# Splitting and reordering the opening of a fused attention and expert kernel: loads, beta, weight scaling, the layout of k and the eps step

## The chip, the cores and the metric

The kernel runs on one core of one Trainium2 chip. A core has a matrix engine (TensorE, "PE" in the profile, with its weight loads as "PEld"), a vector engine (VectorE, "DVE"), an activation engine (ScalarE, "ACT"), a general engine (GpSimd, "POOL") and a queue engine (SyncE, "SP"), which here issues nearly all DMA transfers. Each engine works through its own instructions in order and waits on semaphores of the others. The metric is the device time of one execution in microseconds, median over several runs. Before the change it is 108.06 us (7 runs, 107.44 to 110.72).

## The reference

Two things are computed in a row. First a linear attention with a sketched feature map, for 4 batches of 4 heads with 1088 tokens of 32 values: phi(x) is the outer product of S1 x and S2 x (8 values each, so 64 features).

```python
q_p, k_p = (phi(q), phi(k))
kv = np.einsum('bhsf,bhsd->bhfd', k_p, v)
z = np.sum(k_p, axis=2)
num = np.einsum('bhsf,bhfd->bhsd', q_p, kv)
den = np.einsum('bhsf,bhf->bhs', q_p, z)[..., None] + 1e-06
return (num / den).astype(np.float32)
```

Then the 4352 tokens of 128 values (4 heads side by side) go through one expert of width 2048 with a swish that has a beta for each hidden unit.

```python
h = x @ w_in
g = h * (1.0 / (1.0 + np.exp(-beta * h)))
return (g @ w_out).astype(np.float32)
```

The kernel uses that h · sigmoid(beta h) = silu(beta h) / beta: it multiplies w_in by beta (winp) and w_out by 1/beta (woutp), once, and needs only a plain silu on ACT.

## The kernel before, in words

Tokens lie on partitions in 34 groups t of 32 tokens for each head (32 partitions a head). For k the 34 groups are padded to 36 = 4 x 9, and one DVE or POOL instruction forms the outer products of some of the 9 "outers" j for all heads at once.

**Expert.** `w1` (from L332) makes a wave: four matmuls of 256 tokens, or two of 512, into a PSUM buffer of two banks (pool `psm`, two buffers that take turns), then one ACT silu to g. `w2` (from L308) multiplies g by woutp and sums 16 units of 128 into moeout. The 2048 hidden values are these 16 units. The first 512 tokens go in two chunks of 256, the rest in chunks of 512. A wave of 256 tokens takes four units, so units 8 to 15 are first needed by the third wave.

**Batch 0** is handled by its own path, since nothing can overlap before it. Its q tokens come in two chunks, A (16 groups, the first 512 tokens) and B (18 groups). The steps: `turn_k`, `turn_q` transpose k and q on DVE; `kps` projects k with S1 and S2 on PE; `kab` transposes that back; `outer` forms phi(k) as kp; `gram`, `gram_terms`, `gram_z` build z (in zb0); `kv` sums k_p times v over the 9 outers in KVZ; `spread` on PE makes the repeated a and b factors of q (aps, bps), `asb` copies aps to SBUF on ACT, and `mult` multiplies them to qp on DVE; `den0` makes the denominators dps; `invert` transposes them (dT), adds 1e-6 and takes the reciprocal (rc); `spread_rc` spreads it by a transpose (rb); `num0` makes the numerators nps; `divide0` writes xT, the expert's input. Chunk B repeats spread, mult, den0, invert, num0 and divide0 as the steps aB, bB, mB, dB, iB, nB, xB.

**Weights.** beta is broadcast over the partitions by four PE matmuls with a matrix of ones (L247), copied to beta_bc by ACT (L251), and POOL multiplies w_in by it in eight steps of 256 columns (L258). rbeta = 1/beta comes from a PE transpose and a DVE reciprocal; ACT multiplies w_out by it, unit by unit (L273).

**What sets the order.** Every engine's order is written out by hand: first the straight-line code from L675 to L736, then the string SEQ (L828), whose tokens call small steps: W is a wave, V its second half, tk1, kp1, ka1 and so on are the steps of batch 1. `rest` runs the waves that are left. SP's queue is also in the order of the code: k in two parts, the early q part (chunk A), four loads of v, the first half of w_out and of w_in, the late q part (chunk B), k of batch 1, and the second halves. A DMA issue waits for the one that used the same of eight completion semaphores before it. `gate` is a tiny POOL copy that makes POOL wait for a DVE result before it starts a long multiply. `keep_warm` issues matmuls without use.

Of the kernel before, what the change touches and what calls it, by code (L numbers as in the profile page):

```python
# [9 lines left out]
F32 = mybir.dt.float32  # L10
# [4 lines left out]
P = 128  # L15
# [3 lines left out]
def kernel(  # L19
# [25 lines left out]
    TH = T // 2  # L45
    TPAD = 4 * NJK
    TCH = 512
# [8 lines left out]
    JR = [(0, 2), (2, 4), (4, 6), (6, 9)]  # L56
    WARM0 = 9

# [93 lines left out]

    def load_win(c0, c1):
        nc.sync.dma_start(out=w_in_sb[:, c0:c1], in_=moe_w_in[:, c0:c1])

    def load_wout(j0, j1):
        nc.sync.dma_start(
            out=w_out_sb[:, j0:j1, :],
            in_=moe_w_out[j0 * P : j1 * P, :].rearrange("(j p) m -> p j m", p=P),
        )  # L160
# [5 lines left out]
    load_v(0)  # L166
    load_wout(0, NJ // 2)
    load_win(0, DFF // 2)
    load_rows(q, q_t, 0, "q", ((QA0, T),))
    load_rows(k, k_t, 1, "k")  # L170
    load_win(DFF // 2, DFF)
    load_wout(NJ // 2, NJ)
    load_rows(q, q_t, 1, "q")
# [36 lines left out]
    for n in range(2):  # L210
        qT2.append(sb([P, T, 32], F32, f"qT{n}"))
        kT2.append(sb([P, TPAD, 32], F32, f"kT{n}"))
        nc.gpsimd.memset(kT2[n][:, T:, :], 0.0)
    zb0 = sb([P, H, 32], F32, "zb0")
# [12 lines left out]
    def prep_s(n):  # L227
        st_ = sb([P, 4, R], F32, f"st{n}")
        nc.vector.transpose(out=st_.rearrange("p u r -> p (u r)"), in_=sr[n])
        nc.gpsimd.tensor_tensor(out=sk[:, n], in0=st_[:, :2, :], in1=hm, op=MUL)  # L230
        t = sb([P, R, R], F32, f"s{n}")
        nc.scalar.copy(out=t, in_=cut(st_, ([[1, R], [0, R]], [[0, R], [1, R]])[n]))
        sab.append(t.rearrange("p i j -> p (i j)"))
        if n == 1:
            nc.gpsimd.tensor_tensor(
                out=s2h, in0=cut(sr[1], [[0, H], [1, D]]), in1=cut(mh, [[1, H], [0, D]]), op=MUL
            )


    beta_bc = sb([P, DFF], F32, "beta_bc")  # L240

    bq = [psm.tile([P, 2, 512], F32, tag="wave", name="betaps")]
    bq.append(ps1.tile([P, 512], F32, tag="one", name="betaps"))
    bq.append(pso.tile([P, 512], F32, tag="moeout", name="betaps"))
    for n, t in enumerate((bq[0][:, 0], bq[0][:, 1], bq[1], bq[2])):
# [3 lines left out]
    def beta_out(n):  # L249
        dst = beta_bc[:, (0, 1024, 1536)[n] : (1024, 1536, 2048)[n]]  # L250
        nc.scalar.copy(out=dst, in_=bq[n] if n else bq[0].rearrange("p a b -> p (a b)"))  # L251

# [3 lines left out]

    def prep_win(c0, c1, eng=None):
        (eng or nc.gpsimd).tensor_tensor(  # L258
            out=winp[:, c0:c1], in0=w_in_sb[:, c0:c1], in1=beta_bc[:, c0:c1], op=MUL
        )  # L260

    def prep_rbeta():
        bt = ps1.tile([P, 512], F32, tag="one", name="bt")
# [112 lines left out]


    def turn_k(b, t0=0, t1=T):
        nc.vector.transpose(  # L379
            out=kT2[b % 2][:, t0:t1].rearrange("p t s -> p (t s)"),  # L380
            in_=k_t[b][:, t0:t1].rearrange("p t d -> p (t d)"),
        )

# [8 lines left out]
    def wave2(name):  # L392
        return psm.tile([P, 2, 512], F32, tag="wave", name=name)
# [4 lines left out]
    def one(name):  # L398
        return ps1.tile([P, 512], F32, tag="one", name=name)
# [14 lines left out]
    def kps(b):  # L414
        t = PS["kps"] = two("kps")
        kT = kT2[b % 2]

        project(t, lambda rows, n: kT[rows, :, 8 * n : 8 * n + 8])

# [14 lines left out]
    def kab(b):  # L434
        KAB[b] = turn_ab(PS["kps"], "kab", [[8, NJK], [1, 8], [8 * NJK, 4]])

# [24 lines left out]

    def spread(which, n, dsts):
        t0, tn = q_chk[n]
        for c in range(2):
            for m in range(2):
                for pr, dst in enumerate(dsts):
                    h = 2 * pr + m
                    rows = slice(32 * h, 32 * h + 32)
                    nc.tensor.matmul(  # L469
                        out=dst[64 * c : 64 * c + 64, m, : 32 * tn],  # L470
                        lhsT=(sa if which == "a" else sb_)[rows, :],
                        rhs=qT2[0][rows, t0 + c * tn : t0 + c * tn + tn, :],
                        start=True,
                        stop=True,
                    )

# [58 lines left out]

    def kv(b, j_list):
        for j in j_list:
            for h in range(H):
                nc.tensor.matmul(  # L539
                    out=KVZ[b][32 * h : 32 * h + 32, :F],  # L540
                    lhsT=v_t[b][:, h, j, :],
                    rhs=KP[b][:, j, h, :],
                    start=(j == 0),
                    stop=(j == NJK - 1),
                    skip_group_check=True,
                )


    def gram(b):
        PS["gram"] = t = one("gram")  # L550
# [50 lines left out]

    def invert(dps, nn, tn):
        dT = sbA.tile([P, NJK, 32], F32, tag="dT", name="dT")
        nc.vector.transpose(out=dT[:, :tn].rearrange("p t c -> p (t c)"), in_=dps[:, : 32 * tn])
# [124 lines left out]
    num0(0, nps)  # L729
    keep_warm(2)  # L730
    for c in range(256, DFF, 256):
        prep_win(c, c + 256)
    for j in range(NJ // 2):
        prep_wout_act(j)
    for c in range(2):
        divide0(0, nps, spread_rc(rc, c, 8, 1), c, c + 1)  # L736


    def a_B():
        PS["a"] = [wave2("aps"), two("aps")]  # L740
        keep_warm(2, PS["a"][1][:, 0])
        spread("a", 1, PS["a"])
# [39 lines left out]

    DO = {"W": first, "V": second}
    for i in range(NJ // 4, NJ // 2):
# [9 lines left out]
    for b in range(1, B):  # L794
# [74 lines left out]
```

## Time and profile before

| | |
|---|---|
| median of 7 runs | 108.06 us |
| profiled execution | 108.21 us, span 106.0 us |
| PE busy | 96.4 us (91%) |
| ACT busy | 78.2 us (74%) |
| DVE busy | 66.3 us (63%) |
| POOL busy | 26.3 us (25%) |
| granted PE clock, mean | 0.992 |
| first expert wave starts | 16.91 us |
| first wave of batch 1's tokens starts | 30.88 us |

The page gives one profiled execution; times in the views count from the start of its span. A line of a timeline has the start, the duration, the engine, the source line, the operation, what it writes and reads, and in brackets how long the engine was idle before it and what ended that. A line of the chain of waits has the start, the length and the work that the end depended on at that time; "issue" is time in which nothing visible was waited for. In the rows by shape the columns are: line, engine, operation, output and input with their shapes, count; then busy time and mean nanoseconds of one; then the idle time before them with its releasers. A row of a DMA issue ends in the size of one and the time from issue to landing. PE's matmuls are pipelined, so their durations overlap and a busy PE is not a PE at its peak.

### The profile page before, as it was taken

The numbers are of one execution on the slowest core, as the hardware profiler recorded it, in microseconds if no ns is written. First come the engines' busy times: TensorE is split into PE (matmuls) and PEld (weight loads), VectorE is DVE, ScalarE is ACT, GpSimd is POOL, SyncE is SP. The second block draws the span as 40 slices with busy tenths as digits, with TensorE's granted clock in tenths as the row PEclk, the third lists the DMA queues.
The fourth block names the chain that finished last, engine by engine and source line by source line (L and its number), as shares of the span: only waits on it lengthen the run. The fifth ranks groups of instructions, "written<-read, shape, count | busy, mean of one in ns | idle before, by whom it ended". The sixth has DMA issues, their size and how long they took to land.

```text
span 106.0 us, 2880 instructions
## 1 busy us (share of the span) xinstructions
PE 96.4 (91%) x1175; PEld 46.2 (44%) x1175; DVE 66.3 (63%) x131; ACT 78.2 (74%) x102; POOL 26.3 (25%) x37
## 2 busy tenths in 40 slices
PE   6998966898979999999999999999899999999940
PEld 2335523355546643443454344337344444445720
DVE  5668759499899953997999654879945100200210
ACT  0755185839897985679987199799892999999920
POOL 5410029821059500400670044007400000000000
PEclk9999999999999999999999999999999999999996
DMA  3989999972002300028900463410014041023053
GB/s 79 320 249 301 371 353 386 384 242 69 6 0 50 53 6 0 0 42 117 343 23 12 74 147 89 74 25 6 0 22 77 0 74 31 0 40 62 11 88 50
DMA packets 24580, 11.33 MB, mean 107 GB/s; under 512 B 18900, under 2 KB 23028, under 8 KB 24568
## 3 DMA queue, kind: packets, MB, share of 16 engines
q1 hardware_dynamic: 23808, 11.05, 38.1%
q8 instruction: 9, 0.15, 0.6%
q10 hardware_dynamic: 696, 0.09, 0.5%
q0 software_dynamic: 64, 0.02, 0.1%
q14 instruction: 3, 0.02, 0.1%
HBM read 8.93 MB, written 2.23 MB: 105 GB/s over the span
## 4 chain that ended last, share of the span: by engine, by line
PE 54%; ACT 16%; DVE 11%; DMA 8%; SPq 5%; issue 2%; DVEq 0%; ACTq 0%
PE wave L341 19%; PE moeout L316 19%; ACT g L350 16%; DMA q<-in_q_dram 8%; PE nps L655 4%; PE kvz L539 3%; SPq L134 2%; PE kps L406 2%; PE yps L510 2%; DVE qT L385 2%; PE qps L406 1%; SPq L120 1%; DVE rb L614 1%; DVE xT L634 1%; PE bps L469 1%
## 5 line engine op out<-in xcount | busy, mean ns | idle before, releaser
L350 ACT ACTIVATE g<-wave 128x1024 f16<-128x1024 f32 x68 | 65.1, 1036 | 13.3 <-PE wave L341 13.0
L341 PE MATMUL wave<-xT,winp 128*128 128x512 f16 (+1 forms) x160 | 39.7, 347 | 2.8 <-DVE xT L634 2.2
L316 PE MATMUL moeout<-g,woutp 128*128 128x512 f16 (+1 forms) x160 | 38.6, 347 | 0.3 <-ACT g L350 0.3
L341 PEld LDWEIGHTS <-winp 128*128 128x128 f16 x160 | 14.5, 98 | 19.1 <-issue 9.2
L316 PEld LDWEIGHTS <-woutp 128*128 128x128 f16 x160 | 15.0, 97 | 16.1 <-issue 3.5
L326 DVE STREAM_TRANSPOSE o_sb<-moeout 128x512 f32<-128x512 f32 (+1 forms) x10 | 6.2, 620 | 19.6 <-PE moeout L316 19.6
L445 POOL TENSOR_TENSOR qo<-qab 128x512 f32<-128x512 f32 (+1 forms) x7 | 11.0, 1590 | 20.3 <-DVE qab L534 20.3
L445 POOL TENSOR_TENSOR kp<-kab 128x512 f32<-128x512 f32 (+1 forms) x5 | 6.2, 1250 | 16.8 <-DVE kab L428 9.5
L445 DVE TENSOR_TENSOR kp<-kab 128x512 f32<-128x512 f32 (+2 forms) x11 | 8.9, 820 | 0.0
L456 DVE STREAM_TRANSPOSE qt<-qo 128x512 f32<-128x512 f32 (+1 forms) x12 | 8.6, 742 | 0.0
L666 DVE CAST xT<-nps 128x576 f16<-128x576 f32 x5 | 3.8, 757 | 5.7 <-PE nps L655 2.8
L385 DVE STREAM_TRANSPOSE qT<-q 128x1088 f32<-128x1088 f32 (+2 forms) x5 | 5.3, 1066 | 1.8 <-DMA q<-in_q_dram 1.8
L184 PE MATMUL warm<-idle 128*128 128x512 f16 x13 | 5.4, 556 | 1.1 <-DVE idle L96 1.1
L258 POOL TENSOR_TENSOR winp<-w_in_sb,beta_bc 128x256 f16<-128x256 f32 x8 | 5.6, 732 | 1.2 <-DMA w_in_sb<-in_moe_w_in_dram 1.2
L445 DVE TENSOR_TENSOR qo<-qab 128x512 f32<-128x512 f32 (+1 forms) x5 | 5.8, 1192 | 0.1
L379 DVE STREAM_TRANSPOSE kT<-k 128x1088 f32<-128x1088 f32 (+2 forms) x5 | 5.3, 1067 | 0.7 <-DMA k<-in_k_dram 0.7
L539 PE MATMUL kvz<-kp,v 128*32 128x64 f32 x288 | 5.5, 221 | 0.0
L539 PEld LDWEIGHTS kvz<-kp,v 128*32 128x32 f32 x288 | 4.3, 110 | 2.5 <-issue 1.5
L273 ACT ACTIVATE woutp<-w_out_sb,rbeta 128x128 f16<-128x128 f32 x16 | 5.1, 395 | 0.0
L655 PE MATMUL nps<-qt,nd 32*32 32x288 f32 x192 | 4.8, 412 | 0.0
L428 DVE STREAM_TRANSPOSE kab<-kps 128x288 f32<-128x288 f32 x8 | 3.4, 462 | 1.5 <-PE kps L406 1.5
L486 DVE TENSOR_TENSOR qp<-bps,asb 128x512 f32<-128x512 f32 (+1 forms) x4 | 2.8, 718 | 1.5 <-PE bps L469 1.5
(84 smaller groups left out, 67.2 us busy)
## 6 DMA issues: line engine op xcount, KB each, us to landing
v<-in_v_dram SPq DMA_DIRECT2D x15, 144.0 KB, 4.2
k<-in_k_dram SPq DMA_DIRECT2D x3, 544.0 KB, 6.9
q<-in_q_dram SPq DMA_DIRECT2D x3, 544.0 KB, 7.2
w_out_sb<-in_moe_w_out_dram SPq DMA_DIRECT2D x2, 512.0 KB, 9.0
w_in_sb<-in_moe_w_in_dram SPq DMA_DIRECT2D x2, 512.0 KB, 9.0
out_dram<-o_sb SPq DMA_DIRECT2D x16, 64.0 KB, 1.9
out_dram<-o_sb SPq DMA_DIRECT2D x10, 32.0 KB, 1.6
k<-in_k_dram SPq DMA_DIRECT2D x1, 288.0 KB, 2.8
```

Source lines behind the costliest of these rows:

```text
L184: nc.tensor.matmul(out=t, lhsT=idle, rhs=cut(idle, [[0, 4], [1, P]]), start=True, stop=True)
L258: (eng or nc.gpsimd).tensor_tensor(out=winp[:, c0:c1], in0=w_in_sb[:, c0:c1], in1=beta_bc[:, c0:c1], op=MUL)
L316: nc.tensor.matmul(out=moe["acc"][:, :tw], lhsT=woutp[:, j, :], rhs=g[jj], start=(j == 0), stop=(j == NJ - 1),)
L326: nc.vector.transpose(out=o_sb[:, :nt, :].rearrange("p t d -> p (t d)"), in_=moe["acc"][:, :tw])
L341: nc.tensor.matmul(out=wv[:, jj // per, o : o + tw], lhsT=winp[:, (j0 + jj) * P : (j0 + jj + 1) * P], rhs=xT[:, t0 : t0 + tw], start=True, ...
L350: nc.scalar.activation(out=g[:, :, :gw], in_=wv[:, :, :gw], func=ACTF.Silu)
L379: nc.vector.transpose(out=kT2[b % 2][:, t0:t1].rearrange("p t s -> p (t s)"), in_=k_t[b][:, t0:t1].rearrange("p t d -> p (t d)"),)
L385: nc.vector.transpose(out=qT2[b % 2][:, t0:t1].rearrange("p t s -> p (t s)"), in_=q_t[b][:, t0:t1].rearrange("p t d -> p (t d)"),)
L445: (eng or nc.vector).tensor_tensor(out=cut(dst[b][:, j0:j1], [[F, n], [R, R], [1, R]]), in0=cut(src[b][:, 0, j0:j1], [[R, n], [1, R], [0, ...
L456: nc.vector.transpose(out=QT[b][:, j0:j1].rearrange("p j h c s -> p (j h c s)"), in_=QO[b][:, j0:j1].rearrange("p j h f -> p (j h f)"),)
L539: nc.tensor.matmul(out=KVZ[b][32 * h : 32 * h + 32, :F], lhsT=v_t[b][:, h, j, :], rhs=KP[b][:, j, h, :], start=(j == 0), stop=(j == NJK - ...
L655: nc.tensor.matmul(out=tiles[g // 2][32 * h : 32 * h + 32, g % 2, :JW], lhsT=ND[b][rows, fc, 32 * h : 32 * h + 32], rhs=QT[b][rows, :, h, ...
```

## The change

It changes the first part of the program, batch 0 and the preparation of the weights; the rest of SEQ is as before.

- Loads: w_in and w_out each come as two quarters and a half instead of two halves; the late q part goes ahead of all but the first quarter of w_in.
- k is stored so that the 36 groups are spread over the partitions' outers differently: kT's position is (outer, 32 tokens, quarter), so the transpose writes every fourth element in up to two instructions, and kps and kab read contiguous data.
- beta: two quarters are broadcast after gram in batch 0, two (units 8 to 15) in the new step `be`, after the first wave; their copies are made by ACT and DVE, and the winp steps of units 8 to 15 follow them on POOL.
- Outers: DVE does 0 to 3, 4 to 5 and 6; POOL does 7 and 8; kv takes them in the order 0 to 3, 7, 8, 4, 5, 6, with `den0` in between.
- `invert` of chunk A lets POOL add the 1e-6; between that and the reciprocal DVE does the late q transpose and rbeta.
- w_out units 4 to 7 are scaled by POOL instead of ACT.
- Chunk B's spread of a and one of its copies move ahead of the first wave, the other copy moves from ACT to DVE. Some keep_warm matmuls go, the first group has ten instead of nine. masks and s2h come later.

```diff
-    load_wout(0, NJ // 2)
-    load_win(0, DFF // 2)
+    load_win(0, 1)
     load_rows(q, q_t, 0, "q", ((QA0, T),))
+    load_wout(0, 1)
+    load_win(1, 2)
+    load_wout(1, 2)
     load_rows(k, k_t, 1, "k")
-    load_win(DFF // 2, DFF)
-    load_wout(NJ // 2, NJ)
+    load_win(2, 4)
+    load_wout(2, 4)
...
-        kT2.append(sb([P, TPAD, 32], F32, f"kT{n}"))
-        nc.gpsimd.memset(kT2[n][:, T:, :], 0.0)
+        kT2.append(sb([P, NJK, P], F32, f"kT{n}"))
+        nc.gpsimd.memset(cut(kT2[n], [[P, 2], [4, 32]], 7 * P + 3), 0.0)
...
+    def beta_quarter(n, t):
         row = slice(32 * n, 32 * n + 32)
         nc.tensor.matmul(out=t, lhsT=ones[row, :], rhs=beta4[row, :], start=True, stop=True)
+        return lambda eng=nc.scalar.copy: eng(out=beta_bc[:, 512 * n : 512 * n + 512], in_=t)
...
     def turn_k(b, t0=0, t1=T):
-        nc.vector.transpose(
-            out=kT2[b % 2][:, t0:t1].rearrange("p t s -> p (t s)"),
-            in_=k_t[b][:, t0:t1].rearrange("p t d -> p (t d)"),
-        )
+        t2 = min(t1, 3 * NJK)
+        for c0, c1, ap in (
+            (t0, t2, [[1, (t2 - t0) // NJK], [P, NJK], [4, 32]]),
+            (3 * NJK, t1, [[P, T - 3 * NJK], [4, 32]]),
+        ):
+            if c1 > c0:
+                nc.vector.transpose(
+                    out=cut(kT2[b % 2], ap, c0 // NJK),
+                    in_=k_t[b][:, c0:c1].rearrange("p t d -> p (t d)"),
+                )
...
-        project(t, lambda rows, n: kT[rows, :, 8 * n : 8 * n + 8])
+        project(t, lambda rows, n: kT[rows, :, 32 * n : 32 * n + 32])
...
-        KAB[b] = turn_ab(PS["kps"], "kab", [[8, NJK], [1, 8], [8 * NJK, 4]])
+        KAB[b] = turn_ab(PS["kps"], "kab", [[1, JW]])
...
-    def invert(dps, nn, tn):
+    def invert(dps, nn, tn, eng=nc.vector, between=lambda: None):
...
-        nc.vector.tensor_scalar_add(rv, cut(dT, [[1, nn], [32, tn]]), 1e-6)
+        eng.tensor_scalar_add(rv, cut(dT, [[1, nn], [32, tn]]), 1e-6)
+        between()
         nc.vector.reciprocal(out=rv, in_=rv)
...
     turn_k(0, *K_PARTS[0])
     prep_s(0)
-    masks()
     prep_s(1)
     turn_k(0, *K_PARTS[1])
+    masks()
     sa, sb_ = sab
-    beta_out(0)
-    beta_out(1)
-    w1_ = wave2("aps")
     kps(0)
     turn_q(0, 0, QA0)
-    keep_warm(1, w1_[:, 0])
+    spread_s2()
     w0 = wave2("aps")
-    spread("a", 0, [w1_, w0])
-    asb(0, 0, w1_)
-    asb(0, 1, w0)
-    beta_out(2)
-    rbeta_dve = prep_rbeta()
+    w1_ = wave2("aps")
+    spread("a", 0, [w0, w1_])
+    asb(0, 0, w0)
+    asb(0, 1, w1_)
     kab(0)
-    rbeta_dve()
     gram(0)
-    outer(KP, 0, KAB, "kp", 0, 3)
+    b2 = two("betaps")
+    bq = [beta_quarter(n, b2[:, n]) for n in range(2)]
+    u = [wave2("bps") for _ in range(2)]
+    spread("b", 0, u, ((0,), (1,)))
+    bq[0]()
+    bq[1]()
+    outer(KP, 0, KAB, "kp", 0, 4)
+    gate(KP[0][:, 3, H - 1])
+    outer(KP, 0, KAB, "kp", 7, 9, nc.gpsimd)
     gram_terms()
-    u = [wave2("bps") for _ in range(2)]
-    spread("b", 0, u)
+    gram_z()
     KVZ[0] = pso.tile([P, TCH], F32, tag="moeout", name="kvz")
-    kv(0, range(0, 3))
-    gram_z()
-    outer(KP, 0, KAB, "kp", 3, 6)
-    spare = two("warm")[:, 0]
-    keep_warm(1, spare)
-    kv(0, range(3, 6))
-    keep_warm(1, spare)
-    outer(KP, 0, KAB, "kp", 6, 8)
-    kv(0, range(6, 8))
+    kv(0, range(0, 4), 0, 6)
     mult(0, 0, u[0])
-    outer(KP, 0, KAB, "kp", 8, 9)
     mult(0, 1, u[1])
-    kv(0, [8])
+    outer(KP, 0, KAB, "kp", 4, 6)
+    outer(KP, 0, KAB, "kp", 6, 7)
+    kv(0, (7, 8), 0, 6)
+    dps = one("dps")
+    den0(0, dps)
+    kv(0, (4, 5, 6), 0, 6)
+    rbeta_dve = prep_rbeta(wave2("bt")[:, 0])
     kvd0 = sb([P, 2, F], F32, "kvd0")
     nc.scalar.copy(out=kvd0, in_=cut(KVZ[0], [[0, 2], [1, F]]))
-    gate(KP[0][:, NJK - 1, H - 1])
-    prep_win(0, 256)
-    dps = one("dps")
-    den0(0, dps)
-    turn_q(0, QA0, T)
-    rc = invert(dps, 2, 8)
-    gate(rc)
+    gate(KP[0][:, 6, H - 1])
+    prep_win(0)
+    rc = invert(dps, 2, 8, nc.gpsimd, lambda: [turn_q(0, QA0, T), rbeta_dve()])
+    for j in range(2, NJ // 2, 2):
+        prep_win(j)
...
     num0(0, nps)
-    keep_warm(2)
-    for c in range(256, DFF, 256):
-        prep_win(c, c + 256)
-    for j in range(NJ // 2):
+    rbs = [spread_rc(rc, c, 8, 1) for c in range(2)]
+    for j in range(NJ // 4):
         prep_wout_act(j)
+    for j in range(NJ // 4, NJ // 2, 2):
+        prep_wout_pool(j)
     for c in range(2):
-        divide0(0, nps, spread_rc(rc, c, 8, 1), c, c + 1)
+        divide0(0, nps, rbs[c], c, c + 1)
...
     def a_B():
         PS["a"] = [wave2("aps"), two("aps")]
-        keep_warm(2, PS["a"][1][:, 0])
         spread("a", 1, PS["a"])
...
+    def beta_end(eng):
+        t = two("betaps")
+        for f in [beta_quarter(n, t[:, n - 2]) for n in (2, 3)]:
+            f(eng)
+        for j in range(NJ // 2, NJ, 2):
+            prep_win(j)
...
     SEQ = """
-        W aB c1 V c0 w4 bB W tk1 mB1 mB0 kp1 dB ka1 tq1 V W w5 iB W qp1 gr1 gc1 W V qa1 gw1 gp1
+        aB c1 W C0 be V w4 bB W tk1 mB1 mB0 kp1 dB ka1 tq1 V W w5 iB W qp1 gr1 gc1 W V qa1 gw1 gp1
```

`be` is `beta_end` with DVE's copy; `c1` copies with ACT and `C0` with DVE.

More of the change, by code (lines that the diff above doesn't have):

```diff
@@ L45 @@
     TH = T // 2
-    TPAD = 4 * NJK
     TCH = 512
@@ L56 @@
     JR = [(0, 2), (2, 4), (4, 6), (6, 9)]
-    WARM0 = 9
+    WARM0 = 10
     tok_chk = [(0, 256), (256, 256)]
@@ L151, in load_v, with load_win, load_wout @@
             )
-    def load_win(c0, c1):
-        nc.sync.dma_start(out=w_in_sb[:, c0:c1], in_=moe_w_in[:, c0:c1])
-    def load_wout(j0, j1):
+    def load_win(n, n1):
+        nc.sync.dma_start(out=w_in_sb[:, 512 * n : 512 * n1], in_=moe_w_in[:, 512 * n : 512 * n1])
+    def load_wout(n, n1):
         nc.sync.dma_start(
-            out=w_out_sb[:, j0:j1, :],
-            in_=moe_w_out[j0 * P : j1 * P, :].rearrange("(j p) m -> p j m", p=P),
+            out=w_out_sb[:, 4 * n : 4 * n1, :],
+            in_=moe_w_out[512 * n : 512 * n1, :].rearrange("(j p) m -> p j m", p=P),
         )
@@ L233, in prep_s, with spread_s2 @@
         sab.append(t.rearrange("p i j -> p (i j)"))
-        if n == 1:
-            nc.gpsimd.tensor_tensor(
-                out=s2h, in0=cut(sr[1], [[0, H], [1, D]]), in1=cut(mh, [[1, H], [0, D]]), op=MUL
-            )
+    def spread_s2():
+        nc.gpsimd.tensor_tensor(
+            out=s2h, in0=cut(sr[1], [[0, H], [1, D]]), in1=cut(mh, [[1, H], [0, D]]), op=MUL
+        )
     beta_bc = sb([P, DFF], F32, "beta_bc")
[L242 to L245, printed above, removed]
+    def beta_quarter(n, t):
         row = slice(32 * n, 32 * n + 32)
         nc.tensor.matmul(out=t, lhsT=ones[row, :], rhs=beta4[row, :], start=True, stop=True)
-    def beta_out(n):
-        dst = beta_bc[:, (0, 1024, 1536)[n] : (1024, 1536, 2048)[n]]
-        nc.scalar.copy(out=dst, in_=bq[n] if n else bq[0].rearrange("p a b -> p (a b)"))
+        return lambda eng=nc.scalar.copy: eng(out=beta_bc[:, 512 * n : 512 * n + 512], in_=t)
     winp = sb([P, DFF], F16, "winp")
@@ L255, with prep_win, prep_rbeta @@
     rbeta = sb([P, NJ], F32, "rbeta")
[L257 to L263, printed above, removed]
+    def prep_win(j):
+        c = slice(P * j, P * j + 2 * P)
+        nc.gpsimd.tensor_tensor(out=winp[:, c], in0=w_in_sb[:, c], in1=beta_bc[:, c], op=MUL)
+    def prep_rbeta(bt):
         nc.tensor.matmul(
@@ L378, in turn_k @@
     def turn_k(b, t0=0, t1=T):
-        nc.vector.transpose(
-            out=kT2[b % 2][:, t0:t1].rearrange("p t s -> p (t s)"),
-            in_=k_t[b][:, t0:t1].rearrange("p t d -> p (t d)"),
-        )
+        t2 = min(t1, 3 * NJK)
[7 more added lines that the diff above has]
+                    in_=k_t[b][:, c0:c1].rearrange("p t d -> p (t d)"),
+                )
     def turn_q(b, t0=0, t1=T):
@@ L459, in turn_qo, with spread @@
         )
-    def spread(which, n, dsts):
+    def spread(which, n, dsts, prs=((0, 1),)):
         t0, tn = q_chk[n]
[L464 to L475, printed above, removed]
+        for c, m, pr in [(c, m, pr) for g in prs for c in range(2) for m in range(2) for pr in g]:
+            h = 2 * pr + m
+            rows = slice(32 * h, 32 * h + 32)
+            nc.tensor.matmul(
+                out=dsts[pr][64 * c : 64 * c + 64, m, : 32 * tn],
+                lhsT=(sa if which == "a" else sb_)[rows, :],
+                rhs=qT2[0][rows, t0 + c * tn : t0 + c * tn + tn, :],
+                start=True,
+                stop=True,
+            )
     def asb(n, pr, aps, eng=nc.scalar.copy):
@@ L534, in scale_a, with kv @@
         nc.vector.tensor_tensor(out=a3, in0=a3, in1=cut(rc, [[1, NJK * H], [0, R]]), op=MUL)
-    def kv(b, j_list):
+    def kv(b, j_list, first=0, last=NJK - 1):
         for j in j_list:
@@ L542, in kv @@
                     rhs=KP[b][:, j, h, :],
-                    start=(j == 0),
-                    stop=(j == NJK - 1),
+                    start=(j == first),
+                    stop=(j == last),
                     skip_group_check=True,
@@ L549, in gram @@
     def gram(b):
-        PS["gram"] = t = one("gram")
+        t = PS["gram"] = one("gram")
         for j in range(NJK):
@@ L781, in n_g @@
         num_g(b, PS["nps"])
-    DO = {"W": first, "V": second}
+    def beta_end(eng):
[4 more added lines that the diff above has]
+            prep_win(j)
+    DO = {"W": first, "V": second, "be": lambda: beta_end(nc.vector.tensor_copy), "Be": lambda: beta_end(nc.scalar.copy)}
     for i in range(NJ // 4, NJ // 2):
```

## The prediction, before the result was known

> **What bounds the kernel now.** I read the chain of waits first, in order of time, because the change touches only the first 25 us and the question is whether that stretch lies on the chain at all.
>
> ```profile
> 6.12 8.10 DMA q<-in_q_dram
> 14.22 0.02 issue
> 14.24 0.78 DVE qT L385
> ...
> 16.91 0.60 PE wave L341 x4
> ...
> 20.41 0.77 DVE qp L486
> ...
> 30.88 0.60 PE wave L341 x2
> ```
>
> It does. The second part of batch 0's q is issued at 6.12 us and waited for until 14.22; then a string of VectorE (DVE) work releases the first expert wave at 16.91; then TensorE (PE) and DVE take turns to 20.41, where DVE alone carries the chain to the first wave of batch 1's tokens at 30.88. From there the chain runs through PE's wave and moeout groups, and from 83.9 us through ScalarE's (ACT) g, with no DMA in it. So work up to 20.41 that moves earlier as a block moves the end with it, one for one. Next the timeline of DVE between those points.
>
> ```profile
> 12.04 0.68 DVE L486 TENSOR_TENSOR qp<-bps,asb 128x512 f32<-128x512 f32 x1
> 14.24 0.78 DVE L385 STREAM_TRANSPOSE qT<-q 128x576 f32<-128x576 f32 x1 [1.52 <-DMA q<-in_q_dram]
> 14.94 0.41 DVE L604 STREAM_TRANSPOSE dT<-dps 128x256 f32<-128x256 f32 x1
> 16.43 0.42 DVE L634 TENSOR_TENSOR xT<-nps,rb 128x256 f16<-128x256 f32 x1
> 17.24 0.42 DVE L634 TENSOR_TENSOR xT<-nps,rb 128x256 f16<-128x256 f32 x1
> 17.58 1.30 DVE L379 STREAM_TRANSPOSE kT<-k 128x1088 f32<-128x1088 f32 x1
> 20.41 1.42 DVE L486 TENSOR_TENSOR qp<-bps,asb 128x576 f32<-128x576 f32 x2 [1.53 <-PE bps L469]
> ```
>
> DVE stands idle for 1.52 us because a transpose that nothing needs yet (it serves chunk B) is queued ahead of dT, which was ready since PE ended dps at 13.4. And it idles again for 1.53 us before 20.41, so the stretch 17.24 to 20.41 has room for more DVE work. Third, the DMA issues one at a time: size and time from issue to landing (issued at 4.86, 5.50, 6.72 and 8.44).
>
> ```profile
> w_out_sb<-in_moe_w_out_dram SPq DMA_DIRECT2D x1, 512.0 KB, 7.4
> w_in_sb<-in_moe_w_in_dram SPq DMA_DIRECT2D x1, 512.0 KB, 8.0
> k<-in_k_dram SPq DMA_DIRECT2D x1, 544.0 KB, 9.0
> w_out_sb<-in_moe_w_out_dram SPq DMA_DIRECT2D x1, 512.0 KB, 10.6
> ```
>
> Added up they land at 12.26, 13.5, 15.7 and 19.0, with the late q part at 14.2 between the second and third: in the order of issue, each with its bytes behind the last. Landing goes by the bytes queued ahead. Last, rows by shape that price new work.
>
> ```profile
> L666 DVE CAST xT<-nps 128x576 f16<-128x576 f32 x5 | 3.8, 757 | 5.7 <-PE nps L655 2.8 <-ACT xT L666 2.7
> L648 DVE COPY nd<-ndps 128x256 f32<-128x256 f32 x3 | 1.2, 394 | 0.2 <-PE ndps L587 0.2
> L379 DVE STREAM_TRANSPOSE kT<-k 128x1088 f32<-128x1088 f32 x3 | 3.9, 1296 | 0.0
> L224 DVE TENSOR_REDUCE mk<-ident 128x32 f32<-128x128 f32 x1 | 0.3, 329 | 0.0
> L525 DVE TENSOR_REDUCE rc<-y 128x36 f32<-128x288 f32 x3 | 1.4, 452 | 0.2
> ```
>
> **The change, part by part.** I lay the new start out on the clock of the profiled execution.
>
> *Loads.* Ahead of the late q part there were (KB) k 544, q 256, v 576, w_out 512, w_in 512; now w_out is behind it and w_in ahead is 256. With its own 288 KB it is complete at 1920 KB instead of 2688 KB. The old w_out ended at 1888 KB and landed at 12.26, the old w_in at 2400 KB and 13.5: by that line 12.3 for the new q part. Ends: 14.2 (order does not matter) and 10.0 or earlier (v's last part, 1376 KB, issued at 4.22, landed 4.0 us later); below 12.3 it brings nothing, as DVE is not there sooner (below). I take 12.3. The first w_out quarter ends at 2176 KB, about 13.0; the second quarters at 13.5 and 14.2; k of batch 1 and everything after it has the same bytes ahead as before (15.7, 17.4, 19.0, and q of batch 1 at 20.4). SP issues two more loads of about 0.6 us each ahead of k; each still goes out well before the backlog reaches it (k then at about 8 us for 15.7). q of batch 1 must now wait for the first w_in quarter (near 11.7) before it is issued, and a megabyte of weights is still queued ahead of it.
>
> *PE and DVE to dps.* The four beta matmuls (1.37 us) no longer stand ahead of kps, which can start when kT is written, about 5.45, and ends at 6.2 (0.72); the tenth warm-up matmul ends near 5.5 and costs nothing. masks (0.33 + 0.19) moves behind the second k transpose and ends at 5.85, just before the early q part lands (5.9): hidden by that landing. qT 5.92 to 6.65, kab (0.85) 6.6 to 7.45 instead of 7.99; rbeta (a 0.34 wait and 0.26) leaves the place before the first kp. kp of four units, between 0.90 for 768 elements and twice 0.67, 1.15 us: to 8.65. zt 0.41: to 9.05. PE: aps to 7.5, gram 0.38, two beta quarters 0.7 (half of 1.37), bps 1.0: to 9.6. The two qp multiplies (0.68 each) end at 10.5, kp 512 and 256 (0.67 + 0.41) at 11.5. GpSimd (POOL) takes kp 7 to 9, 1.07 us (1.52 where it ran beside a DVE kp): done by 10.5 and not waited for, since PE does zc (0.63) and units 0 to 3 first. dps 11.1 to 11.8 instead of 13.4; kv, kvd, ndps, nd, nps follow as before (2.05 us from the last kv at 12.25): nps ready at 14.3.
>
> *DVE to the first wave.* dT 11.85 to 12.3; the late qT at 12.35 (its landing now meets DVE, the wait of 1.52 is gone) 0.70; rbeta 0.22; reciprocal 0.25; rb twice 0.87; xT at 14.4, twice 0.8: second xT done at 15.2. The eps step on POOL (nearest rows: 0.22 for its 128x16 multiply) sits behind a winp of 0.73 that needs the first w_in quarter, so it ends near 12.7, under the late qT, which lasts to 13.05. Without that cover it would cost 0.4. The first wave now waits for the second xT too, as its PSUM buffer is the one that holds nps: 15.25 instead of 16.91. Saved: 1.66.
>
> *From the first wave to qp at 20.41.* Chunk B's aps runs ahead of the wave, in PE's idle time (13.9 to 14.8), and both of its warm-up matmuls go. DVE gets the asb copy (row: 757 ns for 576 elements) and two beta copies of 512 (0.68 each, between 394 and 757). The beta matmuls (0.7) wait for ACT's asb copy out of the same buffer, near 15.5, so DVE loses about 0.2: beta done at 17.45. Behind it is queued tk1: two instructions instead of one, 1.30 + 0.07 (the fixed part of a call, 0.13 to 0.15, half hidden): 18.8. bps waits for the beta copies to free its buffer, 17.5 to 18.5, hidden under tk1. So qp starts at 18.8 instead of 20.41: saved 1.6. The cover that was there (1.53 idle) is used up.
>
> *ACT and POOL beside it.* ACT sheds four woutp (1.2 us), an asb and two beta quarters. Its w4 now stands ready at 16.9 but needs the second half of w_out, 19.0, and everything of ACT waits behind it: the second g starts at 19.75 (20.83 before), its moeout matmuls at 20.85, right behind dps (20.8). So this wait is just covered; each 0.1 us that this load lands later costs 0.1. POOL's late winp wait for the second half of w_in (17.4) and end at 20.4; the third and fourth wave need them at 21.3 and 21.8.
>
> *The new k layout.* The transposes write every fourth element, the matmuls and kab read contiguously. kab's strided reading cost nothing (0.46 against 0.46 for qab), so nothing is gained. No row has a strided write. Bounds: 0, and, from reading, mk's 329 ns for 128 elements 128 bytes apart against about 284 on the line of the contiguous row (452 for 288): 0.35 ns an element, 0.38 us a batch, twice on the path. I take 0, since of the two rows kab's has the transpose itself.
>
> [...]
>
> *Costed at nothing.* Seven warm-up matmuls go from PE's stream after the start: the trace shows a granted clock of 1.00 in every microsecond to 22, also over PE's idle 1.69 us before the wave at 16.91, and no gap of the new start is longer. s2h moves behind masks on POOL (0.40, first read at 26). Two woutp on POOL (a winp row is 0.73) end at 16.5 and are first read at 20.9. The kv order changes only which matmul opens and closes the sum.
>
> Sum: 1.66 at the first wave, 1.6 at qp; with the later steps in the same order, 1.65 at the end. The profiled execution took 108.21 for a span of 106.0, so 106.55; it stands 0.15 above the median of 108.06 of the runs shown, and I say **106.5**.
>
> **Rivals.**
> - *A new wait eats part.* The late q part lands at 13.0 instead of 12.3, or the second half of w_out 0.6 later, or strided writes cost their bound (0.75): 107.1 to 107.4. For: three arrivals now meet their users within 0.1 us. Against: bytes ahead of them fix the landings, and they fell or stayed.
> - *The late q lands no earlier* (14.2), if something other than bytes held it: then qT 0.70, rbeta, reciprocal, rb twice and xT twice follow it, first wave at 17.1, and the moved work fits nowhere better: 108.2, no change. Against: the landings in order of issue.
> - *Slower: strided writes at half rate.* 1.05 ns more an element, 1.14 us a batch. The head moves by about 1.0 (0.1 is slack before q), tk1 by 1.14, against 1.65 won: 108.7; tk2 and tk3 stand before kp2 and kp3 in DVE's busiest stretches and could add up to 1.14 each, so 108.7 to 111. It decides from about 0.8 ns an element. [...] Against: the reading rows.
>
> **How the numbers follow.** Forecast (105.7 to 107.0) 0.58; partial gain 0.17, three quarters of it beyond 0.5%; no change 0.11; slower 0.14. About 0.5% (0.54 us) is what a measurement here can tell from none, so faster is under 107.5 and slower over 108.6: 0.71, 0.14, 0.15. The low end is the forecast with another 0.8 (no loss for beta, no wait at w4, and the median's 0.2); the high end takes in no change and stops short of most of the slower case: 105.7 to 108.5.
>
> **What would show it.** Right: no DVE wait on q before dT; the late qT near 12.4; first wave near 15.25; qp of 576 near 18.8; batch 1's first wave near 29.2, and the same 1.6 at every later stage. kT rows of about 0.45 for 288 elements clear the layout, 0.75 convict it. ACT idle before woutp until about 19.0 is the new wait. The forecast fails if the late q part lands after 13, if w_out's second half lands after 19.5, or if DVE between the second xT and qp takes more than 4.5 us instead of 3.6.

## The result

The changed kernel is slower by a little: a median of 108.25 us over 12 runs, against 107.58 us over 31 runs of the kernel before. The ratio is 1.0079, with a 95% interval of 1.0048 to 1.0111. About a quarter of the runs of either kernel are lengthened by 1.5% or more; they count in the medians, but not in the ratios. The prediction was 106.5 us, 1.4% below the 108.06 us then known; its range of 105.7 to 108.5 takes in the measured median, but it said faster.

The two profiled executions alone would have said "no change": 108.10 us (span 105.9) after, 108.21 us (span 106.0) before. The kernel before, as it turned out, was profiled in one of its longer executions, and further runs brought its median down by 0.5 us.

The chain of waits of the changed kernel, in order of time (start, length, work), shows where the saved time went.

```profile
14.57 0.73 DVE xT L635 x2
15.29 0.14 issue
15.43 0.60 PE wave L336 x4
16.02 1.08 PE betaps L246 x4
17.11 0.02 issue
17.13 1.29 DVE beta_bc L247 x2
18.42 0.91 DVE kT L381
19.33 0.58 issue
19.91 0.59 DVE kT L381
20.50 0.60 DVE qp L486
...
30.73 0.61 PE wave L336 x2
```

The 8.10 us wait for the late q is gone from the chain, and the first wave starts at 15.43 us instead of 16.91. But at qp all of it has been given back: 20.50 on this chain, where the chain before stood at 20.41. From the first wave to qp the chain now runs through the two new beta matmuls, their copies and the transpose of batch 1's k. Before, aps, moeout and bps on PE filled that stretch, as the chain of the kernel before has it:

```profile
17.50 0.43 PE aps L184 x2
17.93 0.84 PE aps L469 x16
18.77 0.54 PE moeout L316 x4
19.32 1.00 PE bps L469 x12
```

DVE was idle for the last 1.53 us of it. The timeline of DVE in the changed kernel has the same from the engine's side.

```profile
12.55 0.74 DVE L387 STREAM_TRANSPOSE qT<-q 128x576 f32<-128x576 f32 x1
14.57 0.72 DVE L635 TENSOR_TENSOR xT<-nps,rb 128x256 f16<-128x256 f32 x2
15.21 0.74 DVE L480 COPY asb<-aps 128x576 f32<-128x576 f32 x1
17.13 1.29 DVE L247 COPY beta_bc<-betaps 128x512 f32<-128x512 f32 x2 [1.18 <-PE betaps L246]
18.34 2.17 DVE L381 STREAM_TRANSPOSE kT<-k 128x864 f32<-128x864 f32 x2
20.32 1.43 DVE L486 TENSOR_TENSOR qp<-bps,asb 128x576 f32<-128x576 f32 x2
```

The late qT waits for nothing now, and qp no longer waits for bps. In between stand a new wait of 1.18 us, for the beta matmuls, and a transpose of k that takes 2.17 us where it took 1.30. Its rows by shape:

```profile
L381 DVE STREAM_TRANSPOSE kT<-k 128x864 f32<-128x864 f32 x3 | 5.3, 1761 | 0.0
L381 DVE STREAM_TRANSPOSE kT<-k 128x224 f32<-128x224 f32 x4 | 2.3, 569 | 0.0
L381 DVE STREAM_TRANSPOSE kT<-k 128x576 f32<-128x576 f32 x1 | 1.2, 1204 | 0.8 <-DMA k<-in_k_dram 0.8
```

The row of 576 elements before was:

```profile
L379 DVE STREAM_TRANSPOSE kT<-k 128x576 f32<-128x576 f32 x1 | 0.8, 780 | 0.7 <-DMA k<-in_k_dram 0.7
```

For 576 elements that is 1204 ns against 780: 0.74 ns an element more.

Everything behind batch 1's first wave is a block that only shifts. Over the executions profiled in this study, the time less the start of that wave is 77.3 us:

| profiled execution | late qT starts | first wave | qp of 576 | batch 1's first wave | time | time less that wave |
|---|---|---|---|---|---|---|
| before | 14.24 | 16.91 | 20.41 | 30.88 | 108.21 | 77.33 |
| after | 12.55 | 15.43 | 20.32 | 30.73 | 108.10 | 77.37 |
| before_look2 | 14.03 | 16.70 | 20.13 | 30.59 | 107.90 | 77.31 |
| before_look3 | 13.78 | 16.45 | 19.85 | 30.31 | 107.64 | 77.33 |
| before_new_k | 13.66 | 16.33 | 19.73 | 30.19 | 107.49 | 77.30 |
| before_loads | 12.60 | 15.43 | 19.26 | 29.72 | 107.08 | 77.36 |
| after_again | 12.63 | 15.50 | 20.40 | 30.79 | 108.14 | 77.35 |
| after_old_k | 12.11 | 14.99 | 19.13 | 29.48 | 106.81 | 77.33 |
| after_act_beta | 12.54 | 15.41 | 19.14 | 29.53 | 106.90 | 77.37 |
| after_old_k_act_beta | 12.00 | 14.88 | 18.60 | 29.00 | 106.35 | 77.35 |
| all_early | 11.73 | 14.53 | 17.55 | 28.44 | 105.68 | 77.24 |
| all_early_again | 11.92 | 14.71 | 17.05 | 28.31 | 105.55 | 77.24 |
| all_early_q | 12.54 | 15.33 | 17.89 | 28.29 | 105.55 | 77.26 |

So a variant can be judged by the first 31 us of its profile. From qp to that wave it is 10.35 to 10.47 us in eleven of the thirteen; all_early (10.89) and all_early_again (11.26) differ, and why is said there.

### The profile page after: what moved, and what is told of

It is laid out like the page before. It is cut to its first block, busy times and chain, and to the rows that moved or that the text cites. A ratio compares the mean times of both kernels' runs of the same rounds, so it can differ in the third digit from the quotient of the medians.

```text
span 105.9 us, 2874 instructions
## 1 busy us (share of the span) xinstructions
PE 95.4 (90%) x1169; PEld 45.4 (43%) x1169; DVE 70.1 (66%) x136; ACT 75.5 (71%) x96; POOL 28.9 (27%) x41
## 4 chain that ended last, share of the span: by engine, by line
PE 55%; ACT 16%; DVE 16%; DMA 4%; issue 3%; SPq 1%; POOL 0%; ACTq 0%
PE wave L336 19%; PE moeout L311 18%; ACT g L345 16%; DMA q<-in_q_dram 4%; PE nps L656 4%; PE kvz L539 3%; DVE qT L387 2%; PE betaps L246 2%; PE kps L408 2%; PE yps L510 2%; DVE kT L381 1%; DVE xT L635 1%; DVE qp L486 1%; PE qps L408 1%; DVE beta_bc L247 1%
## 5 line engine op out<-in xcount | busy, mean ns | idle before, releaser
L345 ACT ACTIVATE g<-wave 128x1024 f16<-128x1024 f32 x68 | 65.1, 1037 | 13.7 <-PE wave L336 13.5
L447 POOL TENSOR_TENSOR kp<-kab 128x512 f32<-128x512 f32 (+1 forms) x6 | 7.3, 1217 | 16.9 <-DVE kab L430 9.6
L381 DVE STREAM_TRANSPOSE kT<-k 128x224 f32<-128x224 f32 (+3 forms) x9 | 8.8, 1047 | 0.8 <-DMA k<-in_k_dram 0.8
L447 DVE TENSOR_TENSOR kp<-kab 128x512 f32<-128x512 f32 (+3 forms) x10 | 8.3, 841 | 0.0
L185 PE MATMUL warm<-idle 128*128 128x512 f16 x10 | 4.2, 601 | 1.1 <-DVE idle L95 1.1
L408 PE MATMUL kps<-kT,sk 64*32 64x288 f32 x64 | 2.9, 414 | 2.2 <-DVE qp L486 1.4
L268 ACT ACTIVATE woutp<-w_out_sb,rbeta 128x128 f16<-128x128 f32 x12 | 3.9, 397 | 1.1 <-DMA w_out_sb<-in_moe_w_out_dram 1.1
L480 ACT COPY asb<-aps 128x512 f32<-128x512 f32 (+1 forms) x3 | 1.7, 605 | 3.1 <-PE aps L469 3.1
```

The lines of the kernel that those rows point to most:

```text
L345: nc.scalar.activation(out=g[:, :, :gw], in_=wv[:, :, :gw], func=ACTF.Silu)
L381: nc.vector.transpose(out=cut(kT2[b % 2], ap, c0 // NJK), in_=k_t[b][:, c0:c1].rearrange("p t d -> p (t d)"),)
L408: nc.tensor.matmul(out=t[32 * g : 32 * g + 32, pi, :JW], lhsT=skc[rows, :], rhs=moving(rows, g), start=True, stop=True,)
L447: (eng or nc.vector).tensor_tensor(out=cut(dst[b][:, j0:j1], [[F, n], [R, R], [1, R]]), in0=cut(src[b][:, 0, j0:j1], [[R, n], [1, R], [0, ...
```

## The experiments

My theory after reading the two traces: the gain at the first wave is real, and two costs behind it take it back, the strided write of k and the late beta step on DVE. Both stand in the same stretch. Rivals: one of the two alone is the cause; or something else that varies from run to run.

### The changed kernel again, and each part undone

**after_again** has no edit.

> The changed kernel once more, beside its variants. If the profiled execution is typical: about 0.8% slower than before, first expert wave at 15.4 us, qp of 576 at 20.3 us, and the granted clock near 0.99. If instead it was the fall in the clock (some executions showed 0.98) that made it slower, the slower ones here show the lower clock.

Measured 108.19 us, ratio 1.0071 (1.0031 to 1.0110), first wave at 15.50, qp at 20.40, granted clock 0.993. The slowdown repeats. Two runs at 0.983 took 109.08 and 109.26 us, as the expectation asked, but the lower clock is not the slowdown: six at 0.989 to 0.993 took 107.87 to 108.23, still above the median of the kernel before beside them (107.79). In the runs of the result, three at 0.981 and 0.982 took 109.0 to 109.3; without them the changed kernel is still about 0.6% slower.

**after_old_k** undoes the layout of k.

```diff
-        kT2.append(sb([P, NJK, P], F32, f"kT{n}"))
+        kT2.append(sb([P, 4 * NJK, 32], F32, f"kT{n}"))
...
+        nc.vector.transpose(
+            out=kT2[b % 2][:, t0:t1].rearrange("p t s -> p (t s)"),
+            in_=k_t[b][:, t0:t1].rearrange("p t d -> p (t d)"),
+        )
...
-        project(t, lambda rows, n: kT[rows, :, 32 * n : 32 * n + 32])
+        project(t, lambda rows, n: kT[rows, :, 8 * n : 8 * n + 8])
...
-        KAB[b] = turn_ab(PS["kps"], "kab", [[1, JW]])
+        KAB[b] = turn_ab(PS["kps"], "kab", [[8, NJK], [1, 8], [8 * NJK, 4]])
```

> The changed kernel with kT, turn_k, kps and kab as before. Theory (strided writes): tk1 falls from 2.1 to 1.3 us and qp of 576 starts near 19.6 instead of 20.3, held then by bps, which ends at 19.2; the head gains nothing, since the early part of q lands at 6.36 and sets qT; the end moves by 0.7 to 0.9 us, so about 107.4. Rival (the late beta step alone holds the path): qp stays within 0.2 us of 20.3 and the time stays at 108.2.

Measured 107.17 us, 0.9947 of before (0.9920 to 0.9974) and 1.02 us below after_again. Its DVE timeline:

```profile
5.85 0.70 DVE L381 STREAM_TRANSPOSE qT<-q 128x512 f32<-128x512 f32 x1
...
16.70 1.29 DVE L247 COPY beta_bc<-betaps 128x512 f32<-128x512 f32 x2 [1.18 <-PE betaps L246]
17.90 1.30 DVE L375 STREAM_TRANSPOSE kT<-k 128x1088 f32<-128x1088 f32 x1
19.13 1.38 DVE L480 TENSOR_TENSOR qp<-bps,asb 128x576 f32<-128x576 f32 x2
```

The theory's 0.7 to 0.9 was low, and one part of it was wrong. tk1 gives 0.87 us, as said. But the head gains too: the early qT starts at 5.85 instead of 6.46, and the first wave at 14.99 instead of 15.50. I had read the 6.36 in the chain of the changed kernel as the landing of q. It was the moment DVE came free, after its two slower k transposes and the masks. The wait for the beta matmuls is untouched at 1.18 us.

**after_act_beta** keeps the layout and gives the late beta copies to ACT.

```diff
-        aB c1 W C0 be V w4 bB W tk1
+        aB c1 W C0 Be V w4 bB W tk1
```

`Be` is the same step with ACT's copy.

> The changed kernel with the two late beta copies on ACT instead of DVE; the strided k stays. Theory (DVE waits 1.18 us for the beta matmuls and then has tk1 still ahead of it): tk1 runs from 15.95 to 18.1 under that wait, qp starts when bps ends, near 19.1 instead of 20.3, and the end moves by 1.0 to 1.2 us, to about 107.1. Rival (the strided layout alone costs the time): qp moves by no more than the 0.3 us that bps allows, 107.9.

Measured 106.87 us, 0.9923 of before (0.9895 to 0.9950) and 1.32 us below after_again.

```profile
15.19 0.74 DVE L480 COPY asb<-aps 128x576 f32<-128x576 f32 x1
15.85 2.13 DVE L381 STREAM_TRANSPOSE kT<-k 128x864 f32<-128x864 f32 x2
19.14 1.42 DVE L486 TENSOR_TENSOR qp<-bps,asb 128x576 f32<-128x576 f32 x2 [1.16 <-PE bps L469]
```

qp starts at 19.14, as expected, with the slow tk1 (2.13) hidden in front of a wait of 1.16 us for bps. This one edit of where a copy runs turns a kernel that is 0.7% slower than before into one that is 0.8% faster.

**after_old_k_act_beta** has both edits.

> Both together. Theory: the two share one stretch and are not additive; with the copies on ACT tk1 is hidden in either layout and bps, which waits for the buffer of the beta copies until 18.3, sets qp near 19.1: 106.9 to 107.1, at most 0.2 better than the copies on ACT alone. Rival (two separate costs): the sum of both gains, 1.8 to 2.0, so about 106.3.

Measured 106.80 us, 0.9912 of before (0.9879 to 0.9945), 1.39 us below after_again. The single gains were 1.02 and 1.32, so they are far from additive, as the theory had it: with the copies on ACT, tk1 is hidden in either layout (qp waits 1.16 us for bps behind the strided one, 1.99 behind the other). What is left of the layout's cost is the 0.5 us in the head (first wave 14.88 against 15.41); it shows in the profiles (106.35 against 106.90) and hardly in the medians.

### One part of the change alone, on the kernel before

**before_new_k** adds only the new layout of k to the kernel before (the reverse of the diff above).

> The kernel before with the strided k layout alone. Theory (strided writes cost 0.8 ns an element, but here DVE idles 1.5 us before the late q and 1.5 us before qp, which cover both): kT rows of 1.2 us for 576 and 1.77 for 864 elements, first wave within 0.3 us of before, time 107.6 to 108.0. Rival (the layout costs its 0.9 us a batch wherever it stands, in batches 2 and 3 too): 108.5 or more.

Measured 107.71 us, ratio 0.9984 (0.9935 to 1.0033): no difference. Its DVE timeline:

```profile
5.41 1.05 DVE L385 STREAM_TRANSPOSE kT<-k 128x288 f32<-128x288 f32 x2
...
13.66 0.78 DVE L391 STREAM_TRANSPOSE qT<-q 128x576 f32<-128x576 f32 x1 [0.35 <-DMA q<-in_q_dram]
...
17.01 2.34 DVE L385 STREAM_TRANSPOSE kT<-k 128x864 f32<-128x864 f32 x2
19.73 1.42 DVE L492 TENSOR_TENSOR qp<-bps,asb 128x576 f32<-128x576 f32 x2 [0.39 <-PE bps L475]
```

The transposes are as slow as in the changed kernel, but both idle times of DVE cover them: 0.35 us is left of the one before the late qT, 0.39 of the one before qp. (Not all of the first is the layout's: the four beta matmuls, which stand ahead of kps, took 1.97 us in this execution and 1.37 in the first profile.) The same instructions that cost 1.02 us in the changed kernel cost nothing here that the runs can tell, though the interval leaves room for up to 0.36 us. In batches 2 and 3 they cost nothing either, since the block behind batch 1's first wave keeps its length (77.30 us, against 77.31 to 77.33 of the kernel before).

**before_loads** adds only the new sizes and order of the loads.

```diff
-    load_wout(0, NJ // 2)
-    load_win(0, DFF // 2)
+    load_win(0, 512)
     load_rows(q, q_t, 0, "q", ((QA0, T),))
+    load_wout(0, 4)
+    load_win(512, 1024)
+    load_wout(4, 8)
```

> The kernel before with the changed order and sizes of the weight loads alone; everything else as it was. Theory (the wait for the late q is worth what the chain says): the late q lands at 10.6 to 12.3, the first wave starts near 15.4, bps and qp of 576 follow 1.4 to 1.5 us earlier (18.9 to 19.0), and the time is 106.3 to 106.6. Rival (the loads gain nothing, something else is as late): first wave at 16.9, 107.7.

Measured 107.36 us, ratio 0.9969 (0.9920 to 1.0018): a gain that cannot be told from none, and a miss of my expectation of 106.3 to 106.6.

```profile
12.60 0.77 DVE L387 STREAM_TRANSPOSE qT<-q 128x576 f32<-128x576 f32 x1
...
14.95 0.42 DVE L636 TENSOR_TENSOR xT<-nps,rb 128x256 f16<-128x256 f32 x1
...
16.38 1.24 PE L471 MATMUL aps<-qT,s 32*64 32x288 f32 x16
...
19.26 1.42 DVE L488 TENSOR_TENSOR qp<-bps,asb 128x576 f32<-128x576 f32 x2 [1.86 <-PE bps L471]
```

The late qT starts when DVE reaches it, at 12.60, and the first wave at 15.43 as expected. But qp comes at 19.26, 1.15 us and not 1.5 before that of the first profile. bps sets it, and the lost 0.33 us is in PE's aps between the wave and bps: it took 1.24 us here, against 0.91 in the first profile and 0.75 to 0.84 in the three other profiles of this path (before_look2, before_look3, before_new_k). ACT's asb copies, at 17.67, waited for it. What lengthened it is open. The rest of the miss is the baseline: the expectation was counted from the profile of 108.21 us, 0.6 us above the median.

### How typical was the profile of before?

**before_again**, **before_look2** and **before_look3** are the kernel before, profiled again.

> The kernel before, profiled again. Its first profiled execution took 108.21, over the median of its later runs (107.6 and 107.8), while the changed kernel's profiled executions lie at its median. If the arrival of the late part of q is what varies from execution to execution, this profile shows it landing earlier than 14.2, the first wave earlier than 16.9 by as much, and the span shorter by as much. If not, the late q lands at 14.2 and the span is 106.0 again.

> The kernel before, one more profiled execution. If the late q sets the time, landing and time go together, one for one: 14.2 went with 108.2 us; a landing of 13.5 goes with 107.5, and no landing can bring it below about 106.9, where DVE's own work (its last qp ends at 12.7) takes over. Rival (the spread comes from elsewhere): a time of 107.5 or less with q landing at 14.2.

> The kernel before, another profiled execution, read as the one before it: the start of the late q transpose and the time should differ from the first profile by the same amount.

The profiled execution of before_again took 111.68 us, far above the median of its runs (108.50), and is set aside; its runs gave the ratio 0.9971 (0.9917 to 1.0024) to before, which is itself. The other two, a single execution each, gave 107.90 and 107.64 us. The line of the late q in the second of them:

```profile
13.78 0.78 DVE L385 STREAM_TRANSPOSE qT<-q 128x576 f32<-128x576 f32 x1 [1.36 <-DMA q<-in_q_dram]
```

Late qT at 14.24, 14.03 and 13.78 goes with 108.21, 107.90 and 107.64 us: the differences are 0.46 and 0.57 from first to last. So the profile that I had predicted from had its late q 0.2 and 0.5 us later than two other executions. With a median of 107.58, the usual landing should be near 13.7, and then half a microsecond of the wait was not there to be won in the median; that is a reading of three points, not a count.

### A version that beats both

**all_early** is the changed kernel with k's layout as before, all four beta quarters made by PE and copied by ACT at the start as before, no late beta step (the winp of units 8 to 15 follow POOL's woutp), nine warm-up matmuls in the first group, chunk B's bps right behind the first wave, and w4 behind the second wave.

```diff
-        aB c1 W C0 be V w4 bB W tk1 mB1 mB0 kp1 dB
+        aB c1 W C0 bB V W tk1 mB1 mB0 kp1 w4 dB
...
+    for n, t in enumerate((bq[0][:, 0], bq[0][:, 1], bq[1], bq[2])):
...
-    b2 = two("betaps")
-    bq = [beta_quarter(n, b2[:, n]) for n in range(2)]
```

> The changed kernel with k's layout as before, all four beta quarters early as before, no late beta step, chunk B's bps right behind the first wave and w4 behind the second wave. Theory: with neither the strided k nor the beta step in the stretch, tk1 ends at about 16.9 and qp of 576 starts at 17.0 to 17.5 (18.6 with the late quarters on ACT), and the time is 105.0 to 105.8. Rival (another load takes over): q of batch 1 or the second half of w_out, which lands at 18.1 to 18.2, holds it at 106.3 or more.

> The version with all beta quarters early once more, for its interval: its first profile had the first wave at 14.53, qp of 576 at 17.55 and a span of 103.6. Expected 105.4 to 105.9 us, 1.7% to 2.2% faster than before; if the first measurement was luck of few runs, 106.3 or more.

Measured 105.74 us, ratio 0.9759 (0.9661 to 0.9857), and again, on another chip, 105.55 us, ratio 0.9796 (0.9742 to 0.9849). It makes several changes at once, so no share of the gain can be put down to one of them. The second profile's DVE timeline:

```profile
14.49 0.74 DVE L480 COPY asb<-aps 128x576 f32<-128x576 f32 x1
15.81 1.31 DVE L381 STREAM_TRANSPOSE kT<-k 128x1088 f32<-128x1088 f32 x1 [0.58 <-DMA k<-in_k_dram]
17.05 1.38 DVE L486 TENSOR_TENSOR qp<-bps,asb 128x576 f32<-128x576 f32 x2
18.65 0.85 DVE L430 STREAM_TRANSPOSE kab<-kps 128x288 f32<-128x288 f32 x2 [0.21 <-PE kps L408]
20.27 1.31 DVE L387 STREAM_TRANSPOSE qT<-q 128x1088 f32<-128x1088 f32 x1 [0.78 <-DMA q<-in_q_dram]
```

qp comes 3.3 us before that of the changed kernel, and the rival's other load has begun to hold it: DVE now waits for k (0.58) and q (0.78) of batch 1, so only 2.4 us arrive at batch 1's first wave.

**all_early_q** loads q of batch 1 ahead of the second half of w_out and makes both copies of aps on DVE.

```diff
-    load_wout(2, 4)
     load_rows(q, q_t, 1, "q")
+    load_wout(2, 4)
...
-        aB c1 W C0 bB V W tk1
+        aB C1 W C0 bB V W tk1
```

> all_early with two more moves: q of batch 1 is loaded ahead of the second half of w_out, and both chunk B copies of aps are on DVE, so that bps waits for nothing on ACT. Theory (in all_early, bps waits until 16.65 for ACT, and tq1 then waits 0.37 us for q of batch 1): tq1 starts near 19.2 instead of 20.41 and the time is 104.8 to 105.3. Rival (the second half of w_out, now landing near 20, holds ACT at w4): no gain, 105.6 or more.

Measured 105.27 us, ratio 0.9761 (0.9703 to 0.9819): within the expected range, but its interval overlaps that of all_early, and the reason that I gave did not hold in the profile.

```profile
17.89 1.42 DVE L486 TENSOR_TENSOR qp<-bps,asb 128x576 f32<-128x576 f32 x2 [0.16 <-PE bps L469]
19.53 0.85 DVE L430 STREAM_TRANSPOSE kab<-kps 128x288 f32<-128x288 f32 x2 [0.21 <-PE kps L408]
20.30 1.27 DVE L387 STREAM_TRANSPOSE qT<-q 128x1088 f32<-128x1088 f32 x1
```

q is no longer waited for, but tq1 starts at 20.30, not 19.2. The first wave of this execution came 0.6 us later than in all_early_again (its four beta matmuls, 1.61 us on its chain, stand ahead of kps, and the first kab waited for kps until 7.45 against 6.79), and bps did not start before 17.04. The profile puts that wait down to the first g of ACT, but in all_early_again all sixteen bps were done at 16.67, 0.30 us after its g ended at 16.37, and the last fourteen alone take 0.74 us (all_early): so they went on at about 15.93, before that end. So ACT's copy was not what bps waited for; what it was is open. Which of the two versions is the faster is open too.

## Why the prediction was wrong

- **The chain and the block behind it: right.** What comes before batch 1's first wave moves the end one for one; the 77.3 us of the table show it over 13 profiles. Work up to qp does so too (10.35 to 10.47 us from qp to that wave), as long as no load of batch 1 is waited for behind it.
- **The first wave: right to 0.2 us, in part by luck.** 15.25 was said, 15.43 and 15.50 measured. The late q did not land at 12.3. It was complete by 10.6, as the load's row has it:

```profile
q<-in_q_dram SPq DMA_DIRECT2D x1, 288.0 KB, 5.1
...
w_out_sb<-in_moe_w_out_dram SPq DMA_DIRECT2D x1, 512.0 KB, 9.4
```

  It was issued at 5.50. So the line through the landings of the old loads was too pessimistic; the landing was near the other end that I had named (10.0). That error did no harm, since DVE was not there sooner: DVE, not q, set 12.55. The head was 0.2 us later than I had it, and that is what errors of both signs left: the strided writes, taken at nothing, cost 0.5 (the first wave of after_old_k is at 14.99), and the beta quarters in the head took 0.4 more than said, against steps that were shorter than said (bps took 0.69, not 1.0). The same line of loads put the second half of w_out at 19.0; it landed at 18.2 (8.82 + 9.4), and the wait at w4 (1.13 us on ACT) stayed off the chain.
- **"Two beta quarters 0.7 (half of 1.37)": wrong, and they began late.** Three rows of the changed kernel show both:

```profile
14.30 0.74 PE L469 MATMUL aps<-qT,s 32*64 32x288 f32 x16
15.23 0.64 ACT L480 COPY asb<-aps 128x576 f32<-128x576 f32 x1 [0.40 <-PE aps L469]
15.95 1.13 PE L246 MATMUL betaps<-beta,ones 32*128 32x512 f32 x4
```

  They took 1.13 us, in the head and in the late step alike: 0.43 more than said. The four quarters of the kernel before had run beside each other, each on its own 32 rows: in the first profile all four start within 0.1 us, and their first instructions take 814 to 877 ns each, against 692 for each of the two in the changed kernel. So two are not half of four. And they began at 15.95, not near 15.5: 0.45 more. They wait for ACT's copy of aps, and aps began on PE at 14.30, not at 13.9. The prediction had laid it over nps, which stands ahead of it on PE and by its own sum was not ready before 14.3. The copies could not start before the matmuls ended, so "DVE loses about 0.2" became 1.18. Beta was done at 18.42 instead of 17.45: 0.97 us.
- **The strided writes ("I take 0"): wrong.** The bounds, 0 to 0.38 us a batch, came from rows that read with a stride. The write costs 0.87 us for batch 1's k (2.17 against 1.30), over twice the upper bound: 0.74 ns an element on the row of 576, where 0.8 was named as the point from which the slower rival decides. By the prediction's own terms tk1 ended 0.73 us later than said. 18.8 and 0.97 and 0.73 make 20.5, where the chain has qp. One of the signs of failure that the prediction had named was there: DVE between the second xT and qp took 5.0 us (15.29 to 20.32), over the 4.5.
- **The slower rival: half right.** Half the rate was an assumption, 1.05 ns more an element and 1.14 us a batch; the runs show 0.74 ns and 0.87 us, about three quarters of it. But this does not make the kernel slower alone: after_act_beta keeps the strided writes and is 0.8% faster than before, and after_old_k keeps the beta step on DVE and is 0.5% faster. Only with both is it slower. The prediction had priced each part of that stretch against the 1.53 us of DVE's idle time, and then wrote that this cover "is used up", with nothing in reserve: each later size error went straight to the end.
- **The baseline.** The sum was made against 108.21 us and its late q at 14.24; the median of before is 107.58. So about 0.6 us of the 1.65 that the sum won was not there to be won in the usual execution.
- **eps on POOL: costed at nothing, and 0.15 us.** rc on POOL ended at 13.55 (13.28 and 0.27), not near 12.7, and DVE waited 0.15 us for it. Of the other steps costed at nothing (s2h, woutp on POOL, the order of kv), none stands on the chain from 11 us on.

## What to carry to other kernels

An idle stretch of an engine that sits on the chain can be spent once: price every piece of work that a change puts there at its upper bound, since the first size error in it reaches the end in full, and look for the same work's place on an engine that is idle there (the copies on ACT gained 1.3 us). A cost can be real and free in one kernel and decide in the next: the strided layout cost nothing that could be measured in the kernel before and 1.0 us in the changed one, so a part that was tried alone has to be tried again beside the others. And before predicting from one profile, place it among the runs: here the wait that the change was to remove was 0.5 us longer in that execution than the median lets expect.

## What the runs showed of the hardware

- A DVE transpose of fp32 that writes every fourth element took 1204 ns for 576 elements (after) against 780 written contiguously (before), and 2.13 to 2.34 us for 1088 in two instructions (after_act_beta, after, before_new_k), against 1.30 in one (before). Reading with a larger stride (kab, 288 bytes apart in PSUM) made no such difference: a mean of 462 ns for 288 elements (before), against 457 read contiguously (after).
- Two fp32 matmuls of 512 columns on two different groups of 32 rows took 1.13 us in all seven places that the views show of the changed kernel and its variants (after and after_old_k twice, after_again, after_act_beta and after_old_k_act_beta once). Four on four groups took 1.25 to 1.37 us in three of seven profiles (before_look3, before_loads, before), hardly more, and 1.97 to 2.15 in three others (before_new_k, before_again, before_look2), with 1.61 on the chain of all_early_q; what lengthened those is open.
